# A fused attention and routing kernel: a first chunk of 512 queries, projections with zero-padded weights among the expert products, keys in two halves

## The chip, the cores and the metric

The kernel runs on one core of a Trainium2 chip. The core has a matrix engine (TensorE, PE in the profile; its weight loads are listed apart as PEld), a vector engine (VectorE, DVE), an engine for activations and copies (ScalarE, ACT), a general engine (GpSimd, POOL), and SyncE (SP), which here only issues DMA transfers. Each engine runs its own instructions in the order in which they were written to it, and waits on semaphores where it needs what another one makes. The metric is the device time of one execution in microseconds, as a median over runs.

## The reference, cut to what matters

```python
batch, n_heads, seq, head_dim = 4, 4, 1088, 32      # r = 8
def phi(x):
    a = np.einsum('rd,bhsd->bhsr', S1, x)
    b = np.einsum('rd,bhsd->bhsr', S2, x)
    return np.einsum('bhsi,bhsj->bhsij', a, b).reshape(*x.shape[:-1], r * r)
q_p, k_p = phi(q), phi(k)
kv = np.einsum('bhsf,bhsd->bhfd', k_p, v)
z = np.sum(k_p, axis=2)
num = np.einsum('bhsf,bhfd->bhsd', q_p, kv)
den = np.einsum('bhsf,bhf->bhs', q_p, z)[..., None] + 1e-06
x = (num / den) transposed to (batch * seq, heads * head_dim)      # (4352, 128)

P = exp(x @ w_gate - max)             # 8 experts
8 times: P is divided by its row sums, then by its column sums, then scaled by N / E
out = sum over e of P[:, e:e+1] * (relu(x @ w1[e]) @ w2[e])        # w1: 128 x 1024, w2: 1024 x 128
```

Each token thus has two projections to 8 numbers a head, whose 64 products are its features. The features of keys and values are summed over the sequence; the features of queries meet these sums; the quotient is the input of eight experts, whose outputs are weighted by the routing matrix P.

## The kernel before, in words

Everything is float32. The token axis lies along the free axis of most tiles, and a 128-partition axis holds 4 heads of 32 numbers.

**Attention.** Batch 0 is computed in a way of its own, so that its first results come early; batches 1 to 3 go through `attention(b)`. For batch 0:

- `projections()` makes the weights. S1 and S2 come in as float64 and are made float32 by eleven small DVE instructions; `wd` holds the projection of keys for all heads (block by block, with zeros between heads, `own` being the mask of each head). `repeated(st)` makes `wq` (L264, L265), the projection of queries with each of its 8 numbers repeated to 64, and on POOL `wdq`, the projection for queries of batches 1 to 3.
- `transpose_k(0)` (L293, L295) turns the loaded keys, `keys_ab(0)` (L304, L308) projects them on PE and copies them with ACT to `ab`; `keys_products(0, part)` (L320) multiplies them in three parts on DVE, the first two parts of four row blocks each, and `keys_sums(0)` (L336) sums products times values on PE, over 36 matmuls. `keys_kept(0)` (L352, L354) copies the sums from PSUM to `kvz`, one half on DVE and one on ACT.
- The queries of batch 0 go in three chunks, of 384, 352 and 352. `transpose_q` (L289) turns them. `query_products(c)` (L366, L369) makes two pairs of PSUM tiles: for head pair i, the repeated first and the repeated second projection. It does so in row tiles: the matrix array is split into two halves of 64 rows each, one for each pair of heads, with 64x128 weights. The tiles are the four accumulators `s0` to `s3`, which the expert products use later. ACT copies the first projection to `phs[0]`, and `multiply(c)` (L375) multiplies it on DVE with the second, which is still in PSUM. `fractions(c)` (L384) makes numerators and denominators on PE, and `divide(c)` (L396 to L403) divides on DVE: a transpose, an addition, a reciprocal, a transpose back and a product, into `xT`.
- Batch 1 to 3: `queries_ab(b)` (L419, L422) projects queries on PE, ACT copies them to `qab`, and SP stores these to DRAM (`qa`, `qb`). `repeat_a` (L435) and `repeat_b` (L438) load them back repeated, into `phs` and `rb`; DVE multiplies the two (L445) and PE forms numerators and denominators (L454).

**Experts.** `steps()` is a generator of expert work. One step is a first product (`first`, L894: two matmuls side by side, in column tiles of 64, then a Relu on ACT, L898) together with second products that are due (`into`, L1067), and differences of hidden blocks on DVE (L911, `hb`), which serve a scheme of Strassen's kind. `fill(n)` takes steps from the generator until n units are used up; a unit is a step of 480 tokens, so that a step of 256 counts 0.533. First come groups of unweighted tokens with experts 0 and 1, later all others with the routing weights. PE's part of a step of 256 is two first and about two second matmuls.

**What sets the order.** The order on DVE, PE and ACT is written out by hand at the end of the kernel under `tc.manual_schedule`: first the straight part without expert work, then a part for DVE and PE in which `fill` stands between attention pieces, then `attention(b)` and `routing()` with `fill` between their yields, and then the rest of the generator. ACT, POOL and SP are ordered by a scheduler in the second part, POOL and SP throughout. SP issues the transfers one by one. There are eight completion semaphores for them, taken in turn, so that a transfer is issued only when the eighth one before it has landed.

**PSUM.** `bank()` hands out one of four tiles in turn (`aps`), shared by first products, key projections, key sums, fractions and `queries_ab`. The accumulators `s0` to `s3` are four more.

Of the kernel before, what the change touches and what calls it, by code (L numbers as in the profile page):

```python
# [10 lines left out]
F32 = mybir.dt.float32  # L11
# [39 lines left out]
def kernel(  # L51
# [197 lines left out]
    wq = consts.tile([P, 2, 2, R, R], F32, name="wq")  # L249
    wdq = consts.tile([P, 2, H * R], F32, name="wdq")  # L250
# [10 lines left out]
    def repeated(st):  # L261
        for s in range(2):
            one = half[:, s:s + 1].unsqueeze(2).to_broadcast([P, R, R])
            nc.vector.tensor_tensor(wq[:, 0, s], st[:, 0, 0:R].unsqueeze(2).to_broadcast([P, R, R]), one, op=Alu.mult)  # L264
            nc.vector.tensor_tensor(wq[:, 1, s], st[:, 1, 0:R].unsqueeze(1).to_broadcast([P, R, R]), one,  # L265
                                    op=Alu.mult)


        nc.gpsimd.tensor_copy(wdq[:, 0], wd[:, 0].rearrange("p h r -> p (h r)"))
        nc.gpsimd.tensor_copy(wdq[:, 1].rearrange("p (r h) -> p r h", h=H), wd[:, 1].rearrange("p h r -> p r h"))  # L270

# [10 lines left out]
    load_v(1)  # L282
# [8 lines left out]
    def transpose_k(b):  # L291
        kx = loaded["k", b]
        nc.vector.transpose(out=kT[:, 0:NT * P].rearrange("p (t c s) -> p c t s", c=4, s=32),  # L293
                            in_=kx[:, 0:4 * NT, :].rearrange("p (c t) d -> p c t d", c=4))
        nc.vector.transpose(out=kT[:, NT * P:S], in_=kx[:, 4 * NT:SA, :].rearrange("p a d -> p (a d)"))  # L295

    def keys_ab(b):

        ab = wk.tile([P, 2, NT + 1, H * R], F32, tag="ab", name="ab", bufs=1)
        pk = bank().rearrange("p (t n f) -> p t n f", t=NT, n=2)  # L300
        for t in range(NT):
            for s in range(2):
                sl = slice(64 * s, 64 * (s + 1))
                nc.tensor.matmul(pk[sl, t].rearrange("p n f -> p (n f)"), kT[:, P * t + 64 * s:P * t + 64 * (s + 1)],  # L304
                                 wdf, start=True, stop=True, tile_position=(0, 64 * s))
        nc.scalar.copy(ab[:, :, 0:NT, :], pk.rearrange("p t n f -> p n t f"))
# [49 lines left out]
    chunks = ((0, 384), (384, 736), (736, S))  # L356

    def query_products(c):

        lo, hi = chunks[c]  # L360
        n = hi - lo
        banks = [[mps.tile([P, 512], F32, tag=f"s{2 * i + m}", name="s") for m in range(2)] for i in range(2)]
        for m in range(2):
            for i in range(2):
                sl = slice(64 * i, 64 * (i + 1))
                nc.tensor.matmul(banks[i][m][:, 0:n], wqf[sl, m, :], qT[sl, lo:hi], start=True, stop=True,  # L366
                                 tile_position=(64 * i, 0))
        for i in range(2):
            nc.scalar.copy(phs[0][:, i, lo:hi], banks[i][0][:, 0:n])  # L369
        queries[0, c] = [banks[i][1][:, 0:n] for i in range(2)]  # L370

    def multiply(c):
        lo, hi = chunks[c]
        for i, pb in enumerate(queries[0, c]):
            nc.vector.tensor_tensor(phs[0][:, i, lo:hi], phs[0][:, i, lo:hi], pb, op=Alu.mult)  # L375
# [12 lines left out]
    def divide(c):  # L388
# [6 lines left out]
        rd = wk.tile([P, 384], F32, tag="rd", name="rd")  # L395
        nc.vector.transpose(out=rd[:, 0:n], in_=pd[:, 0:n])  # L396
        rc = wk.tile([P, 12], F32, tag="rc", name="rc")[:, 0:nb]
        nc.vector.tensor_scalar_add(rc, rd[:, 0:n].rearrange("p (b r) -> p b r", r=32)[:, :, 0], 1e-6)
        nc.vector.reciprocal(rc, rc)
        rd = wk.tile([P, 384], F32, tag="rd", name="rd")  # L400
# [63 lines left out]
    def over(b, c):  # L464
        pn = queries.pop((b, c))
        rc = wk.tile([P, 12], F32, tag="rc", name="rc").rearrange("p (t h) -> p t h", h=H)
        nc.vector.reciprocal(rc, pn[:, :, :, D])
        xs = wk.tile([P, 384], F32, tag="rd", name="rd").rearrange("p (h t d) -> p h t d", h=H, t=3)
# [671 lines left out]
    with tc.manual_schedule(engines={engines.DVE, engines.PE, engines.Activation}):  # L1140
        st = projections()
        transpose_k(0)
        keys_ab(0)
# [82 lines left out]
```

## Time and profile before

| | |
|---|---|
| median of 3 runs | 938.18 us (937.0 to 938.84) |
| profiled execution | 934.94 us, span 933.0 us |
| granted clock of PE | 0.998 of full speed |
| PE in 0 to 13.5 us | busy 10.76 us |
| PE in 13.5 to 60 us | busy 44.08 of 46.5 us |
| chain that ended last, by engine | PE 88%, DVE 6%, DMA 2%, issue 2%, ACT 1%, POOL 1% |
| its costliest lines | PE L894 46%, PE L1067 39% |
| expert work starts | 19.90 us (first L894) |

The profile lists for each line of the kernel and each engine the instructions, their mean duration and what they waited for. A float32 matmul shows as two records, so x8 in the profile is four matmuls of the program. Two matmuls in different halves of the array run side by side. Times in the timeline are starts from the beginning of the span.

### The profile page before, as it was taken

What the parts mean: (1) busy time and instruction counts of PE and PEld (TensorE: products, weight loads), DVE (VectorE), ACT (ScalarE), POOL (GpSimd) and SP (SyncE); (2) the same over time, 40 slices, a digit from 0 to 9 for tenths busy, and PEclk for the clock granted to TensorE, in tenths of its full rate; (3) what the DMA queues carried; (4) which work ended last, traced back from release to release, by engine and by line L of the source; (5) the groups of instructions that cost most, each with busy time, mean ns of one, the idle gap of its engine ahead of it and who ended that gap; (6) DMA issues with size and microseconds to landing.
All of it is one profiled execution on the core that took longest, in us unless ns stands there. A gap on an engine that the chain in (4) does not pass through costs nothing.

```text
span 933.0 us, 18870 instructions
## 1 busy us (share of the span) xinstructions
PE 914.5 (98%) x7434; PEld 588.2 (63%) x7434; DVE 693.6 (74%) x1200; ACT 416.9 (45%) x901; POOL 206.2 (22%) x203
## 2 busy tenths in 40 slices
PE   8999899999999999999999999999999999999997
PEld 6666546656666666666666666666666666667885
DVE  8788579887778778585976666965757977768655
ACT  2444345554444454444544444544445444445443
POOL 2011200091655501130020101101110343311210
PEclk9999999999999999999999999999999999999999
DMA  8987100222335545354353534363434556542640
GB/s 229 290 248 214 52 1 1 64 95 81 107 123 168 184 127 162 110 186 131 121 151 132 168 111 145 111 185 128 146 110 152 153 148 196 165 171 91 180 143 12
DMA packets 90728, 128.14 MB, mean 137 GB/s; under 512 B 24352, under 2 KB 68464, under 8 KB 85904
## 3 DMA queue, kind: packets, MB, share of 16 engines
q1 hardware_dynamic: 88240, 123.24, 43.0%
q0 software_dynamic: 1168, 3.54, 1.3%
q8 instruction: 58, 0.95, 0.4%
q10 hardware_dynamic: 1232, 0.16, 0.1%
q14 instruction: 30, 0.25, 0.1%
HBM read 107.88 MB, written 19.05 MB: 136 GB/s over the span
## 4 chain that ended last, share of the span: by engine, by line
PE 88%; DVE 6%; DMA 2%; issue 2%; ACT 1%; POOL 1%; SPq 0%; DVEq 0%; ACTq 0%; POOLq 0%
PE a L894 46%; PE s L1067 39%; DVE hb L911 1%; DMA xd<-xt 1%; POOL xT L480 1%; PE a L336 1%; DMA kx<-in_k_dram 0%; PE a L384 0%; DVE kT L293 0%; DMA ph<-qa 0%; DVE cs L593 0%; PE a L454 0%; PE s L366 0%; DVE kp L320 0%; DVE rs L587 0%
## 5 line engine op out<-in xcount | busy, mean ns | idle before, releaser
L894 PE MATMUL a<-xe,w 128*64 128x256 f32 (+1 forms) x2560 | 525.8, 470 | 0.0
L898 ACT ACTIVATE hb<-a 128x256 f32<-128x256 f32 (+5 forms) x408 | 195.2, 480 | 256.1 <-PE a L894 225.8
L898 ACT ACTIVATE hx<-a 128x256 f32<-128x256 f32 (+1 forms) x360 | 167.2, 465 | 213.4 <-PE a L894 193.8
L894 PEld LDWEIGHTS a<-xe,w 128*64 128x64 f32 x2560 | 220.4, 137 | 65.2 <-issue 1.3
L1067 PE MATMUL s<-hb,ws 128*64 128x256 f32 (+4 forms) x1344 | 241.1, 395 | 1.0 <-DVE hb L911 1.0
L1067 PE MATMUL s<-hx,ws 128*64 128x256 f32 x1280 | 208.7, 379 | 0.2 <-DVE kept L723 0.2
L956 DVE TENSOR_TENSOR hx<-hx 128x512 f32<-128x512 f32 (+1 forms) x204 | 150.1, 745 | 71.2 <-ACT hx L898 66.1
L956 DVE TENSOR_TENSOR hb<-hb 128x512 f32<-128x512 f32 (+1 forms) x204 | 131.0, 653 | 93.4 <-ACT hb L898 89.5
L663 POOL TENSOR_TENSOR xe<-xT,xe 128x768 f32<-128x768 f32 (+2 forms) x41 | 84.0, 2049 | 499.8 <-DMA xe<-pT 474.1
L1067 PEld LDWEIGHTS s<-hb,ws 128*64 128x64 f32 x1344 | 119.6, 137 | 101.9 <-issue 73.7
L1067 PEld LDWEIGHTS s<-hx,ws 128*64 128x64 f32 x1280 | 112.7, 137 | 91.1 <-issue 70.5
L894 PE MATMUL a<-xT,w 128*64 128x480 f32 (+4 forms) x512 | 122.5, 464 | 1.1 <-DVE rd L469 0.9
L1067 PE MATMUL s<-hb,w 128*64 128x256 f32 (+4 forms) x496 | 103.4, 411 | 1.8 <-DVE kept L723 1.8
L911 DVE TENSOR_TENSOR hb<-hb 128x480 f32<-128x480 f32 (+8 forms) x96 | 65.6, 685 | 17.4 <-ACT hb L898 10.2
L1067 PE MATMUL s<-hx,w 128*64 128x256 f32 x384 | 69.3, 379 | 0.0
L894 PEld LDWEIGHTS a<-xT,w 128*64 128x64 f32 x512 | 52.0, 137 | 25.3 <-issue 10.9
L1067 PEld LDWEIGHTS s<-hb,w 128*64 128x64 f32 x496 | 47.8, 137 | 24.2 <-issue 6.5
L239 POOL TENSOR_TENSOR ws<-w 128x256 f32<-128x256 f32 (+1 forms) x70 | 60.0, 893 | 12.7 <-PE a L894 8.2
L911 DVE TENSOR_TENSOR hx<-hx 128x256 f32<-128x256 f32 (+1 forms) x65 | 38.8, 603 | 24.5 <-ACT hx L898 23.4
L956 DVE TENSOR_TENSOR pqg<-hb 128x512 f32<-128x512 f32 x68 | 48.3, 751 | 0.0
L1067 PEld LDWEIGHTS s<-hx,w 128*64 128x64 f32 x384 | 35.9, 137 | 8.6
L956 DVE TENSOR_TENSOR pqg<-hx 128x512 f32<-128x512 f32 x68 | 36.6, 578 | 0.0
(170 smaller groups left out, 480.9 us busy)
## 6 DMA issues: line engine op xcount, KB each, us to landing
w<-in_moe_w_dram SPq DMA_DIRECT2D x82, 512.0 KB, 5.4
ws<-ws SPq DMA_DIRECT2D x34, 1024.0 KB, 4.9
xe<-pT SPq DMA_DIRECT2D x34, 384.0 KB, 4.0
ws<-ws SPq DMA_DIRECT2D x12, 512.0 KB, 3.8
qb<-qab SPq DMA_DIRECT2D x12, 288.0 KB, 4.2
ph<-qa SPq DMA_DIRECT2D x12, 288.0 KB, 5.1
rb<-qb SPq DMA_DIRECT2D x3, 1152.0 KB, 8.2
pb<-pT SPq DMA_DIRECT2D x6, 384.0 KB, 6.7
```

The costliest lines, as they stand in the source:

```text
L239: tc.keep_in_program_order(nc.gpsimd.tensor_tensor(ws[:, c:c + len(ns)], blocks(x), blocks(y), op=Alu.subtract if off else Alu.add))
L336: nc.tensor.matmul(pv[64 * s:64 * (s + 1), i], kp[0:n, H * t + h].rearrange("p i j -> p (i j)"), vx[0:n, slots[h], t, :], start=(t == 0 an ...
L480: nc.gpsimd.dma_start(out=xT[32 * h:32 * (h + 1), b * S:b * S + 4 * W9].rearrange("d (f n) -> d f n", f=4)[:, :, lo:hi], in_=xd.rearrange( ...
L663: tc.keep_in_program_order(nc.gpsimd.tensor_tensor(out, x, pb, op=Alu.mult))
L894: nc.tensor.matmul(ph[sl], loaded_w[j][0][:, P * f + H2 * s:P * f + H2 * (s + 1)], sources[j][:, lo:hi], start=True, stop=True, tile_posit ...
L898: nc.scalar.activation(out=out, in_=ph, func=Act.Relu)
L911: nc.vector.tensor_tensor(out, a, b, op=Alu.subtract)
L956: nc.vector.tensor_tensor(out if not isinstance(out, tuple) else places(*out), places(*a), places(*b) if isinstance(b, tuple) else b, op=A ...
L1067: nc.tensor.matmul(sums[g][i][H2 * s:H2 * (s + 1), n * place:n * (place + 1)], w, x, start=c == 1, stop=c == per, tile_position=(0, H2 * s))
```

## The change

It has four parts, all in the first part of the kernel.

1. `repeated` builds `wq` on POOL, not on DVE, and also builds `wz`: the same repeated projections for each head, with zeros in the rows of the other heads (8 more products of 128x64). `wz` lies in the memory of the tile `xt`, which is used from `attention(1)` on.
2. `transpose_k(0)` and `keys_ab(0)` work in two halves of four row blocks each, with a PSUM tile and an ACT copy for each half. Batches 1 to 3 keep one part.
3. The chunks of queries are 512, 288 and 288. Chunk 0 goes as before, in row tiles to `s0` to `s3`. The others use `wz` in column tiles: for each pair of heads four matmuls over all 128 rows, into two tiles of `bank()`. `query_products` and `multiply` take the pair i as a further argument.
4. The hand-written order is another one. In the straight part only chunk 0 of batch 0 and `queries_ab(1)` are left; `keys_kept(0)` stands ahead of `multiply(0)`. The projections, products, fractions and divisions of the other chunks stand between pieces of expert work of 0.5 units each. `load_k(1)` is issued where `load_v(1)` was; `load_v(1)` follows `queries_ab(1)`, and `load_q(2)` follows `repeat_b(1)`. Up to the key sums of batch 1 the fills add up to 6.25 units, before to 7.5.

```diff
+    wz = wk.tile([P, H, W9], F32, tag="xt", name="xt", bufs=1).rearrange("p h n -> p (h n)")[:, 0:2 * H * R * R]
+    wz = wz.rearrange("p (n h i j) -> p n h i j", n=2, h=H, i=R)
...
     def repeated(st):
+        def repeat(out, column):
+            one = column.unsqueeze(2).to_broadcast([P, R, R])
+            nc.gpsimd.tensor_tensor(out[:, 0], st[:, 0, 0:R].unsqueeze(2).to_broadcast([P, R, R]), one, op=Alu.mult)
+            nc.gpsimd.tensor_tensor(out[:, 1], st[:, 1, 0:R].unsqueeze(1).to_broadcast([P, R, R]), one, op=Alu.mult)
+
         for s in range(2):
-            one = half[:, s:s + 1].unsqueeze(2).to_broadcast([P, R, R])
-            nc.vector.tensor_tensor(wq[:, 0, s], st[:, 0, 0:R].unsqueeze(2).to_broadcast([P, R, R]), one, op=Alu.mult)
-            nc.vector.tensor_tensor(wq[:, 1, s], st[:, 1, 0:R].unsqueeze(1).to_broadcast([P, R, R]), one,
-                                    op=Alu.mult)
+            repeat(wq[:, :, s], half[:, s:s + 1])
...
+        for h in range(H):
+            repeat(wz[:, :, h], own[:, h:h + 1])
...
-    load_v(1)
+    load_k(1)
...
-    def transpose_k(b):
+    def transpose_k(b, parts=((0, NT),)):
         kx = loaded["k", b]
-        nc.vector.transpose(out=kT[:, 0:NT * P].rearrange("p (t c s) -> p c t s", c=4, s=32),
-                            in_=kx[:, 0:4 * NT, :].rearrange("p (c t) d -> p c t d", c=4))
+        for lo, hi in parts:
+            nc.vector.transpose(out=kT[:, 0:NT * P].rearrange("p (t c s) -> p c t s", c=4, s=32)[:, :, lo:hi],
+                                in_=kx[:, 0:4 * NT, :].rearrange("p (c t) d -> p c t d", c=4)[:, :, lo:hi])
...
-    def keys_ab(b):
+    def keys_ab(b, parts=((0, NT),)):
...
+        for lo, hi in parts:
+            pk = bank()[:, 0:2 * H * R * (hi - lo)].rearrange("p (t n f) -> p t n f", t=hi - lo, n=2)
+            for t in range(lo, hi):
...
+            nc.scalar.copy(ab[:, :, lo:hi, :], pk.rearrange("p t n f -> p n t f"))
...
-    chunks = ((0, 384), (384, 736), (736, S))
+    chunks = ((0, 512), (512, 800), (800, S))
 
-    def query_products(c):
+    def query_products(c, i):
...
+        if c == 0:
...
+        else:
+            banks = {i: [bank(), bank()]}
+            for m in range(2):
+                for s in range(2):
+                    nc.tensor.matmul(banks[i][m][64 * s:64 * (s + 1), 0:n],
+                                     wz[:, m, 2 * i + s].rearrange("p i j -> p (i j)"), qT[:, lo:hi],
+                                     start=True, stop=True, tile_position=(0, 64 * s))
+        for j in range(2) if c == 0 else (i,):
+            nc.scalar.copy(phs[0][:, j, lo:hi], banks[j][0][:, 0:n])
+            queries[0, c, j] = banks[j][1][:, 0:n]
...
     with tc.manual_schedule(engines={engines.DVE, engines.PE, engines.Activation}):
         st = projections()
-        transpose_k(0)
-        keys_ab(0)
         repeated(st)
-        load_k(1)
-        transpose_q(0, 0, chunks[0][1])
-        query_products(0)
+        halves = ((0, NT // 2), (NT // 2, NT))
+        transpose_k(0, halves)
+        keys_ab(0, halves)
+        transpose_q(0, *chunks[0])
+        query_products(0, None)
         for part_ in range(3):
             keys_products(0, part_)
         keys_sums(0)
-        multiply(0)
-        transpose_q(0, chunks[0][1])
         keys_kept(0)
+        for i in range(2):
+            multiply(0, i)
+        fractions(0)
         transpose_q(1)
-        query_products(1)
-        fractions(0)
-        multiply(1)
         queries_ab(1)
-        load_q(2)
+        load_v(1)
         repeat_a(1)
         repeat_b(1)
         divide(0)
-        fractions(1)
-        query_products(2)
-        divide(1)
+        transpose_q(0, chunks[0][1])
+        load_q(2)
     with tc.manual_schedule(engines={engines.DVE, engines.PE}):
-        fill(1)
-        multiply(2)
-        fractions(2)
-        fill(1)
+        fill(0.5)
+        query_products(1, 0)
+        fill(0.5)
+        multiply(1, 0)
+        query_products(1, 1)
+        fill(0.5)
+        multiply(1, 1)
+        fill(0.5)
         transpose_k(1)
         load_k(2)
+        fractions(1)
+        fill(0.5)
+        query_products(2, 0)
+        divide(1)
+        fill(0.5)
+        multiply(2, 0)
+        query_products(2, 1)
+        fill(0.5)
+        multiply(2, 1)
+        keys_ab(1)
+        fill(0.5)
+        fractions(2)
+        keys_products(1, 0)
+        fill(0.75)
+        divide(2)
         load_v(2)
         load_q(3)
-        divide(2)
-        fill(1.5)
-        keys_ab(1)
-        fill(1)
-        keys_products(1, 0)
-        fill(1)
         keys_products(1, 1)
-        fill(1)
+        fill(0.75)
         keys_products(1, 2)
-        fill(1)
+        fill(0.75)
         for b in range(1, B):
```

## The prediction

> **What bounds the kernel now.** I read the page's first lines, then busy time by stretch, then PE, DVE and SP in order of time from 5 to 60 us.
>
> ```profile
> PE 914.5 (98%) x7434; PEld 588.2 (63%) x7434; DVE 693.6 (74%) x1200; ACT 416.9 (45%) x901; POOL 206.2 (22%) x203
> ```
>
> TensorE is the bound, so the change is worth the PE idle time it removes less the PE work it adds. The stretches show where idle time can be had (columns: stretch, length, then busy time of PE, PEld, DVE, ACT, POOL):
>
> ```profile
> 0.00:13.50 13.50, 10.76 (x144) 9.30 (x144) 9.94 (x30) 3.28 (x7) 2.61 (x25) 1.00 0.85 247
> 13.50:20.00 6.50, 6.46 (x46) 3.48 (x48) 6.02 (x14) 2.10 (x6) 3.05 (x8) 1.00 0.91 207
> 20.00:36.00 16.00, 15.77 (x206) 10.53 (x208) 12.26 (x23) 6.78 (x19) 0.00 (x0) 1.00 0.98 307
> 34.60:60.00 25.40, 23.25 (x289) 16.48 (x287) 22.16 (x37) 11.37 (x31) 3.96 (x5) 1.00 0.95 265
> ```
>
> From 13.5 us PE hardly stops; in 34.6 to 60 it idles 2.15 us while DVE is busy 22.16 of 25.40. PE in order of time (start, duration, line, tile, count, idle before):
>
> ```profile
> 13.54 1.45 PE L366 MATMUL s<-qT,wq 64*128 64x352 f32 x8 [0.64 <-DVE qT L289]
> ...
> 18.52 1.45 PE L366 MATMUL s<-qT,wq 64*128 64x352 f32 x8
> 19.90 1.22 PE L894 MATMUL a<-xT,w 128*64 128x256 f32 x8
> ...
> 34.61 0.65 PE L894 MATMUL a<-xT,w 128*64 128x256 f32 x4
> ```
>
> L894 at 19.90 is the first expert work; from 13.54 until then PE does projections and fractions. At 34.61 it has finished batch 1's key sums. DVE and SP:
>
> ```profile
> 8.95 2.69 DVE L320 TENSOR_TENSOR kp<-ab 128x1024 f32<-128x1024 f32 x3 [0.70 <-ACT ab L306]
> ...
> 13.42 0.29 DVE L352 COPY kvz<-a 64x128 f32<-64x128 f32 x1
> ...
> 15.96 0.58 DVE L396 STREAM_TRANSPOSE rd<-a 128x384 f32<-128x384 f32 x1
> ...
> 17.72 0.56 DVE L403 TENSOR_TENSOR xT<-a,rd 128x384 f32<-128x384 f32 x1
> ...
> 35.23 0.96 DVE L445 TENSOR_TENSOR ph<-ph,rb 128x768 f32<-128x768 f32 x1 [2.49 <-DMA rb<-qb]
> ```
> ```profile
> SPq L280 <- DMA qx<-in_q_dram: 1.5, 1, 1.5
> ```
>
> The last line is from SP's own waits: its issue at L280 (7.73 us) waited for batch 0's queries, so these landed near 7.65. SP's L172 issue at 10.07 waits in the same way for the fourth value transfer of batch 0.
>
> **Step 1: keys in two halves, `wq` on POOL.** The key transposes (1.25 + 0.20 us) become three (0.58 us for 384 columns and 0.90 for 704 give 1.0 ns a column: 0.7, 0.7, 0.2). Four DVE products for `wq` (about 0.13 us apart, 0.54 us) leave DVE. But the next DVE step, the query transpose, waits for the queries at 7.65 and already started at 7.67. With 512 columns it ends at 8.35 (before: 8.25). The key products then start at 8.3, not 8.95, and end at 10.9. PE's key sums don't gain that: they need the fourth value transfer (10.0), and stand behind L366, now 512 wide: 1.56 us for 384 becomes 2.0, from 8.4 to 10.3. With 2.67 us from the row of L336 they end at 13.0 (before 12.90). So this step brings **nothing**: 0.65 us won on DVE goes into a wait at L352.
>
> POOL gets 4 + 8 products of 128x64. The nearest rows are copies of 128x32 at 0.21 to 0.23 us and a product of 128x256 at 0.73, so 0.25 each: `wq` is ready near 6.4, `wdq` next, the zero-padded weights near 8.6, needed only at 19. Cover: two, four and ten us. The Trainium skill (GPSIMD Engine Reference, Specifications) speaks against it: POOL shares SBUF with VectorE, in contention with two-input DVE operations. This trace has such a place: while POOL added weight sums (44.8 to 48.1), two DVE products of 128x288 took 1.91 us at 46.47, two others 0.95 at 51.45. By the rule up to 0.5 us is lost between 8.3 and 8.6 on the key products; by the rows beside POOL at 15.2 to 18.1 (0.58, 0.56, as elsewhere) nothing. I take 0: the key products have 2 us to spare.
>
> **Step 2: the first chunk.** Before, DVE multiplied chunk 0 while PE summed keys. Now `keys_kept` stands ahead of `multiply(0)`, so DVE idles from 10.9 to 13.0. The two copies (0.26 on ACT, then 0.29 on DVE) end at 13.6, the two products of 512 (0.65 each) at 14.9. Fractions of chunk 0 run on PE from 14.3 to 16.0, `queries_ab(1)` to 17.3; DVE's 1088-column transpose (1.3) ends at 16.1. The division, 15.96 to 18.28 before, has three instructions that grow by 128 columns: 2.32 + 3 x 0.14 = 2.7 us, ending at 18.75. **First expert work 18.75 instead of 19.90**, but PE idles 1.4 us before it, and more attention work is still undone.
>
> **Step 3: the other chunks with zero-padded weights.** 16 matmuls (two halves, chunks of 288) replace 8. In steady state two 256-column matmuls side by side take 0.433 us (L894 at 28.82, L1067 at 29.25), 0.217 a matmul; 288 columns: 0.244. 16 x 0.244 = 3.9 us. Row tiles took 1.45 + 1.38 = 2.83 on the chain of waits. The skill is against this part: TensorEngine Tiling (Array Packing), Performance Considerations, advises two-fold row tiling at a contraction of 64 or less. By that rule what goes is 704 columns at the full pace of two tiles, 8 matmuls of 352 x 0.217/256 = 0.298, or 2.4 us: the edit costs 3.9 - 2.4 = +1.5. Its Tiling Modes section says that a change of mode drains TensorE, which speaks for the edit; the rows have that in them, 2.83 for 2.4, so 0.2 us a chunk. By the rows **+1.1 us**, and these I take.
>
> **The sum on PE up to the end of batch 1's key sums.** Before, from 19.90: fractions of chunk 2, 1.2; 28 + 11 expert matmuls x 0.217 = 8.45; key projections 1.0; key sums 2.45; together 13.1 in 14.7 us, so 1.6 of waits. After, from 18.75: projections 3.9; fractions of chunks 1 and 2, 1.95; 24 + 7 expert matmuls, 6.7; keys 1.0 and 2.45; together 16.0. New waits: for the transpose of the other 576 queries behind the division on DVE (0.25); for PSUM buffers, since projections now take four from the pool of the expert products and are freed by ACT copies and DVE products (0.2 to 1.8 in all, by the 1.6 above). I take 1.2 in all. End: 18.75 + 16.0 + 1.2 = 35.95, **1.35 later** than 34.6, with 8 expert matmuls (1.7 us) fewer done, because the fills add up to 6.25 instead of 7.5. Debt: 3.1 us.
>
> In 34.6 to 60 DVE sets the pace. Work that PE owes can fill part of its 2.15 us of idle; but DVE owes one group of `hb` differences too (1.6 us), so I give back 0.7. From 60 us on both run the same list. **Sum: +2.4 us.**
>
> Queues: on SP `load_v(1)` goes behind the `qa` and `qb` stores (SP waits there for `queries_ab(1)`'s copies: 18.2 instead of 17.85), and `load_q(2)` goes behind `repeat_b(1)`. So ahead of `rb` 0.42 MB of values replace 0.56 MB of queries: `rb` lands near 35 as before, when DVE reaches it. Batch 1's values are needed only at 33, batch 2's queries at 38.5.
>
> The profiled execution took 934.94 us (span 933.0), 3.2 below the median of 938.18. So 937.3 beside the first; against the median **940.6**.
>
> **Rivals.**
> - *DVE's stretch pays for all.* If the finer interleaving makes no new waits (-1.2) and the owed work fills all 2.15 us of idle instead of 0.7 (-1.45), the sum is -0.25: 937.9. For it: 25.40 - 23.25 really is idle, and `kept` and `rd` end it. Against: DVE is 87% busy there. It decides if DVE is not behind at 36 us.
> - *`rb` comes late.* Five issues of values (0.46 us each) stand ahead of the repeat loads, 2.3 us, and are not made up by the later `load_q(2)`: DVE waits at L445 until 36.7 or so, and PE behind it: +1.5, 942.1. For it: L445 already waits 2.49. Against: the bytes.
> - *The edit does less than it says:* POOL holds DVE up (step 1) and the drain was dearer than 0.2 us a chunk. With 0.5 lost and 0.9 more won the forecast becomes 940.2.
>
> **Chances.** Forecast 0.6 (own range 939 to 942.2), first rival 0.22, second 0.14, third 0.04. About 0.2% (1.9 us) separates a difference from none: the forecast lies just past it. Faster 0.1 (the first rival's lower part, with a run spread of 1.8), same 0.3, slower 0.6. Range 937.8 to 942.9.
>
> **What would show it.** Key sums ending at 12.9 to 13.1; first expert matmul at 18.6 to 18.9 with 1 to 1.5 us idle before it; projections of about 0.97 us each; batch 1's key sums ending near 36; L445's first at 35 to 36. It is wrong if PE is dense before 18.7, if PE's idle time in 36 to 60 falls below 1 us, or if waits in 18.75 to 36 are below 0.5.

## The result, and the profile after

The changed kernel took **939.87 us** (median of 4 runs, 937.72 to 940.15), the kernel before 937.86 beside it (4 runs, 937.0 to 938.84): a ratio of **1.0016**, 95% interval 0.9998 to 1.0034, so +1.5 us with a range from -0.2 to +3.2. By the 0.2% bound that is no difference that this measurement can tell. The profiled execution of the changed kernel took 937.72 us (span 935.9), 2.8 more than the profiled one before (934.94, span 933.0). The executions of the kernel before are of two kinds: of 35 beside later runs, 17 had a mean granted clock of 0.998 or more (median 935.1 us) and 18 a lower one (median 937.4), and its profiled execution is of the first kind.

The page's first line of busy times, and the stretches of the changed kernel (columns as before: stretch, length, busy time of PE, PEld, DVE, ACT, POOL, then granted clock, DMA share, GB/s):

```profile
PE 918.1 (98%) x7450; PEld 563.4 (60%) x7450; DVE 693.0 (74%) x1197; ACT 416.6 (45%) x902; POOL 208.1 (22%) x215
```
```profile
0.00:13.50 13.50, 11.99 (x144) 10.37 (x144) 8.14 (x24) 3.65 (x8) 5.59 (x37) 1.00 0.84 240
13.50:20.00 6.50, 4.39 (x28) 2.42 (x30) 5.80 (x10) 1.08 (x3) 3.03 (x8) 1.00 0.45 139
20.00:36.00 16.00, 15.97 (x214) 12.60 (x212) 11.73 (x25) 6.39 (x17) 0.00 (x0) 1.00 0.86 250
34.60:60.00 25.40, 22.38 (x295) 16.61 (x293) 19.60 (x36) 10.24 (x28) 3.96 (x5) 0.93 0.94 267
```

Two things are new. In 13.5 to 20 PE now idles 2.1 us, and the DMA share is 0.45 where it was 0.91. In 34.6 to 60 PE idles 3.0 us where it idled 2.15, and its clock is 0.93, not 1.00. PE in order of time shows the places; only its rows with an idle time in front are copied:

```profile
14.46 2.01 PE L402 MATMUL a<-ph,kvz 128*64 128x512 f32 x7 [1.48 <-DVE ph L393]
...
18.89 0.65 PE L912 MATMUL a<-xT,w 128*64 128x256 f32 x4 [1.02 <-DVE xT L421]
...
40.70 1.20 PE L472 MATMUL a<-kvs,ph 128*64 128x66 f32 x24 [2.88 <-DVE kvs L362]
```

The first two are the straight part: fractions waiting for the products, and the first expert matmul waiting for the division. The third is the first use of batch 1's products, `tops(1, 0)`. VectorE at the same places:

```profile
7.75 0.71 DVE L296 STREAM_TRANSPOSE qT<-qx 128x512 f32<-128x512 f32 x1 [0.43 <-DMA qx<-in_q_dram]
...
13.32 0.29 DVE L362 COPY kvz<-a 64x128 f32<-64x128 f32 x1 [2.09 <-ACT kvz L364]
...
37.91 0.96 DVE L463 TENSOR_TENSOR ph<-ph,rb 128x768 f32<-128x768 f32 x1 [2.50 <-DMA rb<-qb]
```

VectorE sat 2.09 us for the key sums' first copy, and at 37.91 it had waited 2.50 for `rb`; before, the same product started at 35.23. PE's 2.88 at 40.70 is the end of that chain (`kvs` is named because that copy stands just ahead on VectorE).

To see where time is lost and won back, I follow PE's program by landmarks. At each one the **debt** is the landmark's start in one kernel less its start in the kernel before, plus the expert work that the kernel before had done by then and the other had not, at the pace of packed expert matmuls in the traces (four 256-column instructions in 0.43 us). Span differences are the last column:

| kernel | batch 1's key sums (32-40 us) | first tops (38-45) | batch 2's key sums (59-69) | batch 3's key sums (85-96) | routing's second step (129-143) | span |
|---|---|---|---|---|---|---|
| changed | +2.97 | +5.39 | +6.03 | +5.21 | +1.99 | +3.0 |

So the change owes 3 us at 33, 6 us at 66, then **wins 4 us back** between 66 and 136, and loses another 1.0 to the end. The forecast had the first number and a sum that is near, but not the two in between. Which causes they have is what the runs are for.

### The profile page after: what moved, and what is told of

Read it like the earlier page. It is cut to its first block, busy times and chain, and to the rows that moved or that the text cites. A ratio compares the mean times of both kernels' runs of the same rounds, so it can differ in the third digit from the quotient of the medians.

```text
span 935.9 us, 18917 instructions
## 1 busy us (share of the span) xinstructions
PE 918.1 (98%) x7450; PEld 563.4 (60%) x7450; DVE 693.0 (74%) x1197; ACT 416.6 (45%) x902; POOL 208.1 (22%) x215
## 3 DMA queue, kind: packets, MB, share of 16 engines
q0 software_dynamic: 1168, 3.54, 1.3%
## 4 chain that ended last, share of the span: by engine, by line
PE 86%; DVE 9%; DMA 2%; issue 1%; SPq 1%; ACT 1%; POOL 0%; DVEq 0%; ACTq 0%; POOLq 0%
PE a L912 45%; PE s L1085 38%; DVE hb L929 3%; DMA rb<-qb 1%; PE a L114 1%; DMA xd<-xt 1%; DVE hb L974 1%; PE a L346 1%; SPq L172 0%; ACT hb L916 0%; DVE ph L463 0%; SPq L448 0%; DVE rs L605 0%; POOL xT L498 0%; PE a L437 0%
## 5 line engine op out<-in xcount | busy, mean ns | idle before, releaser
L912 PE MATMUL a<-xe,w 128*64 128x256 f32 (+1 forms) x2560 | 519.5, 470 | 0.0
L912 PEld LDWEIGHTS a<-xe,w 128*64 128x64 f32 x2560 | 208.3, 137 | 76.9 <-issue 1.3
L974 DVE TENSOR_TENSOR hx<-hx 128x512 f32<-128x512 f32 (+1 forms) x204 | 157.0, 779 | 71.2 <-ACT hx L916 65.8
L1085 PE MATMUL s<-hx,ws 128*64 128x256 f32 x1280 | 206.0, 379 | 0.0
L1085 PEld LDWEIGHTS s<-hb,ws 128*64 128x64 f32 x1344 | 113.7, 137 | 104.8 <-issue 77.4
L1085 PEld LDWEIGHTS s<-hx,ws 128*64 128x64 f32 x1280 | 106.7, 137 | 96.5 <-issue 73.5
L1085 PEld LDWEIGHTS s<-hb,w 128*64 128x64 f32 x496 | 45.7, 137 | 24.9 <-issue 9.6
L974 DVE TENSOR_TENSOR pqg<-hb 128x512 f32<-128x512 f32 x68 | 44.5, 695 | 0.0
```

What stands on the lines that cost most here:

```text
L912: nc.tensor.matmul(ph[sl], loaded_w[j][0][:, P * f + H2 * s:P * f + H2 * (s + 1)], sources[j][:, lo:hi], start=True, stop=True, tile_posit ...
L974: nc.vector.tensor_tensor(out if not isinstance(out, tuple) else places(*out), places(*a), places(*b) if isinstance(b, tuple) else b, op=A ...
L1085: nc.tensor.matmul(sums[g][i][H2 * s:H2 * (s + 1), n * place:n * (place + 1)], w, x, start=c == 1, stop=c == per, tile_position=(0, H2 * s))
```

## The experiments

Each kernel ran 6 to 12 times beside runs of the kernel before (median 936.4 to 936.6 in these comparisons); ratios are to those.

| run | median | ratio, 95% interval | batch 1's key sums | first tops | batch 2's key sums | batch 3's key sums | routing's second step | span |
|---|---|---|---|---|---|---|---|---|
| e1 values early | 934.77 | 0.9985, 0.9974-0.9997 | +2.96 | +3.32 | +2.22 | +1.41 | -1.92 | -0.7 |
| e2 products first | 938.07 | 1.0013, 1.0002-1.0025 | +2.71 | +6.84 | +7.03 | +6.21 | +2.89 | +4.0 |
| e3 row tiles | 938.18 | 1.0021, 1.0011-1.0030 | +2.15 | +8.86 | +9.48 | +8.66 | +5.02 | +6.1 |
| e4 before, new load order | 940.37 | 1.0045, 1.0030-1.0060 | -0.82 | +3.98 | +4.32 | +4.33 | +6.20 | +7.4 |
| e5 before, new pace | 935.17 | 0.9986, 0.9973-0.9998 | +0.34 | +3.70 | +3.70 | +2.89 | -0.76 | +0.3 |
| e6 = e1, old pace | 939.37 | 1.0033, 1.0020-1.0045 | +7.54 | +7.23 | +6.44 | +6.44 | +6.33 | +6.2 |
| e7 = e1 + e2 | 933.48 | 0.9971, 0.9958-0.9984 | +1.74 | +2.55 | +1.52 | +0.71 | -2.68 | -2.2 |
| e8 keys in one part | 938.75 | 1.0023, 1.0012-1.0035 | +4.20 | +6.95 | +7.33 | +6.52 | +3.24 | +4.0 |
| e9 before, pace later | 930.98 | 0.9940, 0.9924-0.9956 | -0.17 | -0.17 | -0.88 | -1.77 | -5.52 | -4.7 |
| e10 changed, old pace | 940.24 | 1.0041, 1.0026-1.0056 | +5.57 | +5.26 | +5.14 | +5.13 | +6.72 | +7.4 |
| e11 all in | 932.10 | 0.9954, 0.9938-0.9969 | +1.11 | +0.80 | +0.30 | -0.31 | -3.65 | -3.1 |
| e12 = e11, padded | 934.65 | 0.9984, 0.9974-0.9995 | +3.54 | +3.23 | +2.58 | +1.96 | -1.05 | -0.7 |

The debts come from one profiled execution each, and one thing moves between executions: when batch 0's queries land. VectorE's transpose of them started between 7.5 and 9.6 us over these fourteen profiles, though nothing ahead of it differs much; at 7.75 in the changed kernel's. Where that matters, the difference is taken off and said.

**The late `rb`.** Two runs ask whether the order of SP's issues makes it: e1 takes the values out of the queue in the changed kernel, e4 puts only the new load order into the kernel before.

```
# e1: changed kernel
     load_k(1)
+    load_v(1)
...
         queries_ab(1)
-        load_v(1)
         repeat_a(1)
```

> The changed kernel with the values of batch 1 (five issues on SP) sent at the start, behind batch 1's keys, and no longer behind batch 1's query factors. Theory (the lost time in 36 to 60 comes from SP's queue: five issues of v, measured 3.98 + 0.91 us in the changed kernel's trace, stand ahead of the factor repeats): qb's repeats start about 4.9 us sooner, rb lands at 33 to 35 in place of 37.9, VectorE no longer waits 2.50 us for rb, PE's idle 2.9 us at 37.8 to 40.7 and the granted clock of 0.50 after it go, and the debt at the first tops falls from 5.4 to about 3. If nothing later absorbs it the time falls by 2 to 3.3 us against the changed kernel (about 935 to 936); if the later waits only shift, by less than 1. Rival (rb is late because the query factors themselves are late, ScalarE's copy of qab, or because the transfers are slow): rb still lands at 37 or later, time within 0.5 us of the changed kernel.

```
# e4: kernel before
-    load_v(1)
+    load_k(1)
...
         repeated(st)
-        load_k(1)
...
         queries_ab(1)
-        load_q(2)
+        load_v(1)
...
         divide(0)
+        load_q(2)
```

> The kernel before with only the order of loads of the changed one: batch 1's keys at the start, batch 1's values behind batch 1's query factors, batch 2's queries behind the division of chunk 0. Nothing else of the change. Theory (the late rb is the load order's doing alone): rb lands 2.5 to 3.5 us later than in the kernel before, VectorE waits for it by name, PE idles 2 to 3 us near 37 with a lower granted clock behind it, and the debt at the first tops is 2 to 3.5 us with a debt under 0.5 at batch 1's key sums; the end is 0 to 3 us slower. Rival (the late rb comes of the products and key sums being late by the change's own 3 us): rb lands within 1 us of the kernel before, time within 0.5 us of it.

First SP's queue in the changed kernel, in order of time (start, the time its issues took, line, transfer, count):

```profile
19.63 3.64 SPq L448 DMA_DIRECT2D qb<-qab  x4
23.31 3.98 SPq L172 DMA_DIRECT2D v<-in_v_dram  x3
27.34 0.91 SPq L176 DMA_DIRECT2D v<-in_v_dram  x2
28.29 2.60 SPq L453 DMA_DIRECT2D ph<-qa  x4
30.93 0.58 SPq L456 DMA_DIRECT2D rb<-qb  x1
```

The five value issues hold the queue from 23.31 to 28.25, 4.9 us, and `rb` goes out at 30.93; before, one query issue of 1.31 us stood there and `rb` went out at 27.56. VectorE's first use of `rb` in e1, and then in e4:

```profile
35.84 0.96 DVE L464 TENSOR_TENSOR ph<-ph,rb 128x768 f32<-128x768 f32 x1 [0.44 <-DMA rb<-qb]
```
```profile
39.77 0.96 DVE L445 TENSOR_TENSOR ph<-ph,rb 128x768 f32<-128x768 f32 x1 [7.48 <-DMA rb<-qb]
```

In e1 `rb` is issued at 27.92 and is there at 35.8: a little later than the 33 to 35 expected, but the wait is gone, the debt at the first tops falls from 5.39 to 3.32, and at batch 2's key sums from 6.03 to 2.22. The time falls by 0.31% against the changed kernel's ratio, about 2.9 us. In e4 the load order alone brings 4.8 us of debt between batch 1's key sums and the first tops, more than expected: VectorE waits 7.48 us there and PE 5.0. The rivals (late factors, late products) are out: the load order is the cause and is enough by itself.

The second half of the loss is the clock. PE's granted clock in the changed kernel, in steps of 2 us (eighth value of a row: the granted clock, after the POOL column):

```profile
38.00:40.00 2.00, 0.00 (x0) 0.00 (x0) 1.93 (x4) 0.00 (x0) 0.00 (x0) 1.00 1.02 337
40.00:42.00 2.00, 1.30 (x30) 1.30 (x32) 1.94 (x4) 0.00 (x0) 0.00 (x0) 0.79 1.14 207
42.00:44.00 2.00, 2.00 (x12) 1.11 (x12) 0.86 (x1) 0.38 (x1) 0.00 (x0) 0.50 0.97 256
44.00:46.00 2.00, 2.00 (x19) 1.49 (x17) 0.77 (x2) 0.73 (x2) 0.00 (x0) 0.85 0.86 263
```

After 2.88 us without a matmul PE runs at half clock for some 3.4 us: 2 x (0.21 + 0.50 + 0.15) = 1.7 us of lost clock. In e1, where PE waits 0.8 us at most, the whole stretch from 36 to 60 has 1.00. So the 3.8 us that e1 saves up to batch 2's key sums are 2.1 of wait and 1.7 of clock.

**The 4 us won back.** Every run with 6.25 expert steps ahead of batch 1's attention wins 4.0 to 4.5 us between 60 and 140, whether it is late or not; e4, with 7.5, wins nothing. What PE waited for from 60 to 140, before and then changed (engine, waiting line, releaser, us, times, longest):

```profile
PE a L488 <- issue: 2.5, 1, 2.5
PE s L1067 <- DVE kept L723: 1.6, 1, 1.6
...
PE a L454 <- ACT m L735: 0.6, 1, 0.6
```
```profile
PE a L506 <- DMA xT<-xd: 1.0, 1, 1.0
PE s L1085 <- DVE kept L741: 0.7, 1, 0.7
```

The waits for the last batch's tokens at the logits and for `kept` are shorter by 2.4 us; all waits there add up to 5.7 us before and 2.7 after. So 3.0 of the 4.0 us are waits with a name; the other 1.0 is not traced. (`kept` holds sums of expert outputs, which VectorE makes out of the accumulators.) Is it the place of the expert steps against the attention, which the smaller fills shifted by 1.25 steps? Four runs:

```
# e5: kernel before
         divide(2)
-        fill(1.5)
+        fill(0.25)
         keys_ab(1)
```
```
# e6: in e1; e10: in the changed kernel
         keys_products(1, 2)
-        fill(0.75)
+        fill(2.0)
```

> The kernel before with one number changed: the third fill in the interleaved part is 0.25 in place of 1.5, so that 6.25 and not 7.5 expert steps are handed out before batch 1's attention, as in the changed kernel. Theory (the 3.3 us that the changed kernel wins back between 60 and 140 come of the place of the expert steps against the attention and the logits, PE's waits of 2.5 us for xT at the logits and 1.6 us for kept becoming 1.0 and 0.7): debt near 0 (within 0.6) up to batch 2's key sums, then -2 to -4 at 130 to 140, and a span of 929 to 931.5, 0.2 to 0.4% faster than the kernel before. Rival (the give-back comes of something else in the change, or of being late itself): span within 0.7 us of 933.0, the waits of 2.5 and 1.6 us stay.

> The run with batch 1's values sent at the start, and the last fill before batch 1's attention 2.0 in place of 0.75, so that 7.5 expert steps are handed out as in the kernel before. Theory (place of the expert steps): the late give-back goes, the debt stays at 2 to 3.4 from 60 to 175, PE's waits of 2.5 us at the logits and 1.6 us for kept are back, span 935 to 936.5, 3 us more than the 932.3 of that run. Rival: span within 0.8 us of 932.3.

> The changed kernel with the last fill before batch 1's attention 2.0 in place of 0.75, values still sent late. Theory: 1.25 more steps are 2.1 us of PE work in front of the first tops, so PE's wait for rb falls from 2.9 to about 1 and the clock stays at 1.00: debt 3 to 4 at 60 in place of 6.2; but the late give-back of 3.7 us goes too, so that the debt stays at 3 to 4 to the end: span 936 to 937.5, no faster than the changed kernel's 935.9. Rival (pace does not matter to rb's wait, or the give-back stays): PE idle over 2 us at 38 to 42, or debt under 1 at 135.

```
# e9: kernel before
-            for n, _ in zip((1.4,) * (9 if b + 1 < B else 5), attention(b), strict=True):
-                fill(n)
+            for i, (n, _) in enumerate(zip((1.4,) * (9 if b + 1 < B else 5), attention(b), strict=True)):
+                fill(n - 1.25 if (b, i) == (1, 8) else n)
```

> The kernel before with the 1.25 expert steps taken out behind batch 1's attention (its last fill 0.15 in place of 1.4) and not ahead of it. Theory (two effects of the place of the expert steps: ahead of batch 1's attention they cover the arrival of rb, from batch 2 on they only shift against the attention and win 3.5 to 4 us at 65 to 140): debt 0 within 0.5 up to batch 2, PE's wait for rb under 0.5 us, then -3 to -4 at 130, span 929 to 930.5, 0.25 to 0.4% faster than before. Rival (the give-back needs the early lateness, so that loads of later batches are there): span within 1 us of 933.0.

e5 wins 4.5 us back from 60 to 140, as the theory has it, and its waits there fall to 0.8 and 0.7 us, but it misses the expected span (933.3, by its letter the rival's): with fewer steps in front of it, batch 1's attention comes too early for `rb`. VectorE waits 5.28 us for it, and PE:

```profile
PE a L454 <- DVE kvs L352: 3.8, 1, 3.8
```

Behind that wait the clock fell to 0.50 too, from 39.5 to 42.9. So the 1.25 steps were also the cover of `rb`. e9 keeps that cover and takes the steps out behind batch 1's attention. Its waits in 60 to 140, and its stretches:

```profile
PE a L488 <- DMA xT<-xd: 0.7, 1, 0.7
PE s L1067 <- DVE kept L723: 0.7, 1, 0.7
PE a L304 <- DVE kT L295: 0.6, 1, 0.6
```
```profile
60.00:100.00 40.00, 39.26 (x532) 28.64 (x530) 33.83 (x65) 18.57 (x47) 5.65 (x10) 1.00 0.60 173
100.00:190.00 90.00, 87.62 (x556) 47.67 (x554) 73.61 (x130) 46.21 (x95) 13.78 (x19) 1.00 0.11 32
```

PE's busy time there was 38.47 and 85.16 in the kernel before. With one number changed the kernel before gains 4.7 us of span and 0.6% of its time: **930.98 us, the fastest kernel of the study**. It was expected at 929 to 930.5 of span and came to 928.3. All six executions of e9 had a mean clock of 0.998 or more, so the difference of the medians, 5.4 us, also holds what half of the old kernel's executions lose by a lower clock. That they lose it at the 2.5 us wait at the logits is likely by the last section, but not shown: none of them was profiled.

e6 and e10 are the test in the other direction. In neither does the debt fall behind batch 2's key sums (e6: 6.44 there, 6.33 at routing's second step; e10: 5.14, then 6.72): the give-back is gone, as expected, and PE's waits of 2.2 us at the logits and 1.6 us for `kept` are back. Their level was missed: 2 to 3.4 was expected for e6 and 3 to 4 for e10. In e6's profile the queries landed 1.9 us later than in the changed kernel's, and its first expert matmul came 3.5 later; in e10 1.0 and 1.5. In e6 the other 1.6 us are the clock's: PE had waited so long for the queries that it then ran at 0.50. Its projection, and the stretch at half clock:

```profile
10.49 2.98 PE L379 MATMUL s<-qT,wq 64*128 64x512 f32 x8 [2.65 <-DVE qT L297]
11.34:14.75 3.41, 3.41 (x32) 1.75 (x30) 1.57 (x3) 1.07 (x2) 0.00 (x0) 0.50 1.06 339
```

In the changed kernel the same projection took 1.99 us, and the key sums behind it 2.46 where e6 has 3.06. In e10 the other 0.5 us arise in the division, as in e8 below. The rest, 1.1 us in each, is the place where I put the steps: from batch 1's key projections to its key sums the debt grows by 1.68 us in e6, e10 and e12 alike and by 0.58 in the changed kernel. With 1.25 steps in one gap the second products wait for `hb`, which is 0.5 us of it; the other 0.6 is not traced. e10 is no faster than the changed kernel (ratios 1.0041 and 1.0016, intervals overlapping), as expected. PE's wait for `rb` vanished there though VectorE still waited 2.0 us for it. At the logits e10 shows another fall of the clock:

```profile
120.50 3.38 PE L506 MATMUL a<-xT,wg 128*32 128x512 f32 x18 [2.23 <-DMA xT<-xd]
```
```profile
117.52:120.93 3.41, 1.18 (x14) 0.31 (x12) 0.00 (x0) 0.00 (x0) 1.13 (x3) 1.00 0.22 58
120.94:124.34 3.40, 3.40 (x18) 1.17 (x11) 1.62 (x3) 0.00 (x0) 0.00 (x0) 0.50 0.00 0
```

That is the step from 5.1 to 6.7 in its debt, and in e4 the one from 4.3 to 6.2.

**The copy ahead of the products** (step 2 of the prediction). e2 and e7 turn two lines round, e2 in the changed kernel, e7 in e1:

```
         keys_sums(0)
-        keys_kept(0)
         for i in range(2):
             multiply(0, i)
+        keys_kept(0)
```

> The changed kernel with the first chunk's two products on VectorE ahead of the copy of batch 0's key sums (kvz). Theory of the prediction's step 2 (VectorE idles from 10.9 to 13.0 because the copy stands before the products): the idle stretch is used, the products (1.2 us together) are off the path, and the first expert matmul comes 1.0 to 1.3 us sooner than 18.89, at about 17.7; the end moves by -1.2 if it isn't absorbed. Rival (the products wait for the projection's banks or ScalarE's copies anyway, and delay kvz): first expert matmul within 0.3 us of 18.89.

> Both edits that helped in the changed kernel: batch 1's values sent at the start, and the first chunk's products ahead of the copy of the key sums. Theory: the products' 1.2 us leave the path between key sums and the first expert matmul, less the 0.7 that the fractions then wait for kvz: first expert matmul 0.5 to 1.0 sooner at the same landing of q, rb in time (VectorE waits under 1 us for it), and the time 0.5 to 1.0 us under the run with the early values alone, at about 934. Rival (a later wait swallows it): within 0.4 us of that run.

By its letter e2 fell to the rival (first expert matmul 18.64, 0.25 sooner), but its queries landed 0.84 later. e7 and e1 had them within 0.1 us of each other. The row of the first expert matmul in e1, and then VectorE's products and copy in e7 with its first expert matmul:

```profile
18.88 0.65 PE L913 MATMUL a<-xT,w 128*64 128x256 f32 x4 [1.21 <-DVE xT L422]
```
```profile
10.97 1.27 DVE L394 TENSOR_TENSOR ph<-ph,s 128x512 f32<-128x512 f32 x2
13.19 0.29 DVE L363 COPY kvz<-a 64x128 f32<-64x128 f32 x1 [0.95 <-ACT kvz L365]
```
```profile
17.67 0.65 PE L913 MATMUL a<-xT,w 128*64 128x256 f32 x4 [1.22 <-DVE xT L422]
```

1.21 us sooner, and 1.22 less debt at batch 1's key sums; the medians differ by 1.3, with overlapping intervals. Some 0.2 us of this are not the order's: a small VectorE instruction of the division took 0.37 us in e1 and 0.17 in e7. So the idle stretch that the prediction named is real, and the products moved into it, 1.27 us long, are worth about 1.1. In e2 the gain was lost again: PE's wait for `rb` grew to 4.6 us.

**The form of the projections** (step 3). e3 projects chunks 1 and 2 in row tiles in the changed kernel. e11 does so with everything that helped (e7, the old pace ahead of batch 1, e9's later cut); e12 is e11 with the padded form back. In row tiles both pairs of heads are projected at once, into the accumulators `s0` to `s3`, so the place of the second pair and the PSUM tiles change with the form:

```
# e3, e11: query_products
-        if c == 0:
+        if i == 1:
+            return
+        if True:
...
-        else:
-            banks = {i: [bank(), bank()]}
...
-        for j in range(2) if c == 0 else (i,):
+        for j in range(2):
```

> The changed kernel with the chunks 1 and 2 projected in row tiles as the first is (four matmuls a chunk with 64 rows each, both pairs of heads at once, into the four banks of the straight part) in place of eight zero-padded column-tile matmuls. Theory of step 3 (the padded form costs PE 3.9 us against 2.83 in row tiles): PE's time in the projections falls by 1.1 to 1.9 us and the debt at batch 1's key sums falls from 2.97 to between 1.1 and 1.9. Rival (row tiles keep expert matmuls from overlapping, as a drain before and after each group, and hold the four banks that the experts want): debt at batch 1's key sums stays within 0.5 us of 2.97 or grows.

> The run with early values and products first, with chunks 1 and 2 in row tiles, the last fill before batch 1's attention 2.0 and batch 1's last fill 0.15. Theory (row tiles are worth 1.4 us at batch 1's key sums, the fill covers rb and the 1.25 steps come out later): debt 0 to 0.7 at batch 1's key sums in place of that run's 1.74, no wait for rb above 0.5, then -2.5 to -3.7 at 140: span 929.5 to 930.5, about that of the kernel before with the steps taken out later, so that the rest of the change is worth nothing. Rival (row tiles pay for nothing, as the wait for rb takes it): span 930.7 or more.

> The run with everything in, but chunks 1 and 2 in the zero-padded column tiles of the change again; nothing else differs. Theory (prediction's step 3: the padded form costs PE 1.1 us more, 3.9 in place of 2.83): the debt at batch 1's key sums rises by 1.0 to 1.6 from 1.11, stays that much higher, and the span is 1 to 1.6 us over 929.9. Rival (the projection's form is hidden behind VectorE's work and the expert matmuls between): debt and span within 0.5 us of that run.

PE in e11 and then in e12; each projection is followed by its next row, so that its length is the difference of the starts:

```profile
18.57 1.24 PE L381 MATMUL s<-qT,wq 64*128 64x288 f32 x8
19.74 1.52 PE L908 MATMUL a<-xT,w 128*64 128x256 f32 x12
```
```profile
19.14 1.19 PE L385 MATMUL a<-qT,xt 128*64 128x288 f32 x8
20.14 0.63 PE L913 MATMUL a<-xT,w 128*64 128x256 f32 x4
...
23.80 1.39 PE L385 MATMUL a<-qT,xt 128*64 128x288 f32 x8
25.03 0.60 PE L913 MATMUL a<-xT,w 128*64 128x256 f32 x4
```

A chunk in row tiles takes 1.17 us, both chunks 2.34; in the padded form the four pieces take 1.00, 0.97, 1.23 and 1.21, together 4.41. That is 2.07 us more on PE, and some 0.5 of it are waits: the two pieces of chunk 2 take 0.25 us longer than those of chunk 1. In them the fifth instruction, the first into the second PSUM tile, starts 0.45 us after the third; the other pieces have 0.24. In the changed kernel, whose four pieces also add up to 4.41, these fifth instructions start 0.04 us after a Relu of ACT and the division's last product on VectorE have ended, which free PSUM tiles. The view of that line names the two, with the idle time of the weight loads (us, times):

```profile
L384 PE MATMUL a<-qT,xt x32: 406/406/457, 19.7 to 27.0; 128*64 128x288 f32 x32
  DVE xT L421: 0.5, 1
  ACT hb L916: 0.5, 1
```

In the debt at batch 1's key sums e12 stands 2.43 above e11. Its first expert matmul already came 0.49 later (18.37 after 17.88: queries 0.74 later, division 0.25 shorter), so 1.9 are the form's, and 1.8 in the span (2.3 less 0.5). The medians differ by 2.5, and the intervals of the ratios don't overlap. That is somewhat more than the 1.0 to 1.6 expected, and the rival is out. In e3 the same 1.9 us are won up to batch 1's key sums (2.15 beside 2.97, with the first expert matmul 1.13 later), and then lost: `rb`, 9.5 us on its way in that profile, is there only at 41.4, and PE waits 7.2 us. e11's debt at batch 1's key sums was 1.11 (0 to 0.7 expected), its span 929.9, as expected, and its 932.10 is no faster than e9's 930.98.

**Keys in halves** (step 1):

```
-        halves = ((0, NT // 2), (NT // 2, NT))
+        halves = ((0, NT),)
```

> The changed kernel with batch 0's keys in one part (one transpose of 1024 columns, one bank of key factors, one copy) and all else as changed. Theory (prediction's step 1: the halves are worth nothing, since the products then wait for other data): batch 0's key sums end within 0.3 us of 12.98, debt after that as in the changed kernel, time within 1 us of it. Rival (the halves are worth their 0.65 us on VectorE): key sums end at 13.4 to 13.7 and everything after is 0.5 to 0.7 later.

The key sums end at 13.67, in the rival's range by its letter. But VectorE in e8 shows why:

```profile
8.43 0.71 DVE L296 STREAM_TRANSPOSE qT<-qx 128x512 f32<-128x512 f32 x1 [1.05 <-DMA qx<-in_q_dram]
```

It had finished the keys at 7.38 and waited 1.05 us for the queries; the transpose starts 0.69 later than in the changed kernel, and the key sums end 0.69 later. Whatever the halves do is hidden by that wait. (Its further 0.5 us of debt arises in the division, where one VectorE instruction on 16 columns took 0.73 us, and 0.18 in the changed kernel; the last section returns to it.) The medians cannot tell the two apart (ratios 1.0023 and 1.0016, intervals overlapping).

## Why the prediction came out near, and where it was wrong

The forecast of +2.4 us stands beside +1.5 measured (interval -0.2 to +3.2) and +2.8 in the profiled execution. By its own steps:

- **Step 1, "nothing": right.** Key sums ended at 12.98 (12.9 to 13.1 said). The 0.65 us that left VectorE turned into a wait: 0.43 for the queries, more at L362. POOL's work on the padded weights cost VectorE nothing, but only by its place: the key products took 2.69 us, as before, and POOL's last product (8.38 to 8.67) met them for 0.13 us. In e1, e7 and e11, where they started ahead of it (8.15 to 8.25), they took 2.79 to 2.92 us, and that product 1.27 where it takes 0.29. So the contention that was set at 0 is real.
- **Step 2: right.** VectorE idle for 2.09 before the copy, first expert matmul at 18.89 (18.75 said) with 1.02 of PE idle right before it. e7 shows that the stretch is worth about 1.1 us.
- **Step 3, "+1.1 us": right, with its waits under another name.** The padded form took 4.41 us of PE, not 3.9, but 0.5 of that are the waits for PSUM buffers, which the prediction had among its 1.2 us of waits; 3.9 are left. The 2.83 of before adds a duration (1.45) to a distance of starts (1.38); by starts alone it is 2.76, so the form costs +1.1. The Trainium skill's TensorEngine Tiling (Array Packing), Performance Considerations, which asks for row tiles at a contraction of 64, was worked out to +1.5 with row tiles at full pace, 2.4 us: of the two values weighed, that of the rows was the nearer. The advice itself holds here, as e11 and e12 show: 2.34 us in row tiles, 4.41 padded. Key sums of batch 1 ended at 35.88 (35.95 said), and **the debt there was 2.97 against a forecast of 3.1**.
- **"`rb` lands near 35 as before": wrong.** This is the step that failed first. The queue was weighed by its bytes, but SP's issues take time themselves: five value issues took 4.9 us, not the 2.3 of the second rival, and the query issue that left took back only 1.3. VectorE had `rb` at 37.9, outside the 35 to 36 that the prediction named as its sign. The rival had the mechanism and the place; its +1.5 was too small, as e1 shows 2.1 us of wait and 1.7 of clock, which nothing in the forecast allowed for.
- **"I give back 0.7" in 34.6 to 60: wrong in sign**, by the same cause. PE lost 3.1 us there.
- **"From 60 us on both run the same list": wrong.** It is the same work, but the fills hand out 6.25 and not 7.5 steps ahead of batch 1's attention, so every piece of attention behind that comes with 1.25 fewer expert steps done ahead of it. I counted the 8 matmuls as owed and didn't ask what their new place does to the waits at the logits and for `kept`: 4.0 us in the changed kernel's debts, 4.7 in e9's span.

So the forecast's sum is near by luck, because two large errors cancel: about +3.8 that it missed in 36 to 60 (3.1 lost where 0.7 was to be won), and about -3.0 that it missed from 60 to the end. It was also carried from one profiled execution to the median as if the 3.2 us between them were a constant. But the four runs before (937.0 to 938.8 us) lie where its executions of lower clock do (936.3 to 939.8), and its profiled execution does not; what the change does to that share was not asked. With the old pace the changed kernel is 0.41% slower than the kernel before (e10, 3.8 us, of which about 1.1 by the ledger come from putting the 1.25 steps into one gap). The parts that cost are shown one by one: the late `rb`, the copy ahead of the products, the padded projections. With all three mended and the new pace (e11, 0.9954) the new structure still doesn't beat the old one with that pace (e9, 0.9940).

What stays open: why the order of steps from 60 on is better by just this shift (only two places were tried); the up to 1.2 us that several of these kernels lose against the kernel before after routing's second step; why `rb` took 6.9 us from issue to landing in the changed kernel's profile and 8.8 to 9.5 in e2, e3 and e4; and the spread of the queries' landing.

## What to carry to other kernels

Weigh a moved load by the time its issues hold the queue, read from the rows in that place of the queue, and ask what goes out behind it. When a change shifts how much filler work is handed out before some stage, treat the new place of all filler behind it as a change of its own: run the old kernel with just that shift, since it can be worth more than the edit (here 0.6% for one number). And when a forecast comes out right, look at it by landmarks: a sum can be right while two of its terms are wrong.

## What the runs showed of the hardware that was not expected

**The clock falls after less idle time than the skill says, where that lies in one window.** The Trainium skill (TensorE: Matmul & The Clock Gate, Part 1) has PE's clock halved after at least one idle window of about 3.4 us. Here it fell to 0.50 after 2.88 us of idle (changed kernel, 40.70) and after 2.23 us (e10, 120.50), while the 2.50 us that the kernel before waits at its logits left it at 1.00. The page also says that its window runs free of the program, and the fourteen traces agree. In each of them the changes of the granted clock lie whole multiples of 3.41 us apart, and each stretch at 0.50, but for one at the very end, lasts 3.41 or 6.83 us. Cut into such windows, the traces have, ahead of that end, eleven with 2.23 us or more without a matmul, and the clock was 0.50 in the window behind every one of them; no other window has more than 1.69 us, and behind none of those did it fall. The windows at the logits of the kernel before:

```profile
110.46:113.86 3.40, 2.46 (x14) 0.53 (x10) 1.08 (x2) 0.57 (x1) 2.20 (x4) 1.00 0.19 43
113.87:117.28 3.41, 1.86 (x18) 0.66 (x18) 1.01 (x2) 0.00 (x0) 0.00 (x0) 1.00 0.06 14
```

Its 2.50 us lie across a boundary, 0.95 and 1.55; e10's 2.23 lie in one window. So the window is as long as the page says, but it need not be idle throughout. The price is half a window, 1.7 us, for each window at 0.50: by these runs a wait of 2.2 us on TensorE costs 1.7 us more or nothing, as it falls.

**VectorE and POOL hold each other up.** The division's small second instruction (12 or 16 columns) took 0.17 to 0.18 us in six of the profiles and 0.23 to 0.73 in eight, and in each of these eight it ended 0.02 to 0.03 us after an instruction of POOL. In e11 the two end at 15.99 and 15.97:

```profile
15.51 0.48 DVE L412 TENSOR_SCALAR rc<-rd 128x16 f32<-128x16 f32 x1
15.24 0.73 POOL L202 TENSOR_TENSOR ws<-w 128x256 f32<-128x256 f32 x1
```

That is the 0.5 us of the division in e8 and e10: POOL adds up expert weights and fills a tile there, and VectorE's instruction ends when POOL is done.

**An issue's length is not the same everywhere.** Three value issues of the same form took 3.98 us at 23.31, 1.33 each, in the changed kernel; the prediction had taken 0.46 from quieter rows. Their neighbours were long too, whatever they carried: the last `qb` store ahead of them took 1.45 us, and in the kernel before the query load in that place 1.31. What sets the length was not tested.
